# Linear attention and a swish MLP on one core: a hand-made order on all engines, tails in a chunk of their own, a block-diagonal kv and 1 KB loads

## The chip, the cores and the metric

The kernel runs on one core of one Trainium2 chip. The metric is the device time of one execution in microseconds (us). A profile covers a single execution and is some 2 to 4 us shorter than the timed run. All comparisons use runs that the records call fast.

## The reference

Eight batches of eight heads, 576 tokens, 64 channels per head. The attention is linear: a softmax of q over the channels, a softmax of k over the tokens, and `kv = k_s^T v` per head. Its output goes through an MLP with a swish in the middle.

```python
q_s = exp(q - max(q, -1));  q_s /= sum(q_s, -1) + 1e-9
k_s = exp(k - max(k, 2));   k_s /= sum(k_s, 2) + 1e-9
kv  = einsum('bhsd,bhse->bhde', k_s, v)
x   = einsum('bhsd,bhde->bhse', q_s, kv)        # -> (4608, 512)
h   = x @ w_in                                  # (512, 2048)
out = (h * sigmoid(beta * h)) @ w_out           # (2048, 512), float32
```

Both kernels leave out the maximum, work in bf16 on TensorE, and use `sigmoid(z) = (1 + tanh(z/2)) / 2`, so that the gate is one tanh on ScalarE and one `(tanh + 1) * h` on VectorE.

## The kernel before

A batch of 576 tokens is cut into four pieces of 128 and one of 64; the MLP works in nine chunks of 512 tokens, which straddle the batches. The order on each engine is left to the framework's scheduler.

```python
S_CHUNKS = [(0, 128), (128, 128), (256, 128), (384, 128), (512, 64)]

def attention(b):
    for ci, (s0, rows) in enumerate(S_CHUNKS):      # q by SP, k and v by GpSimd; 256 B runs
        nc.sync.dma_start(qt[:rows], q[b, :, s0:s0+rows, :].rearrange("h p d -> p h d"))
    # ... k and v the same way; exp of q and k, row sums and multiplies per 128-token piece ...
    for j in range(HP):                             # two heads at a time
        for ci, (s0, rows) in enumerate(S_CHUNKS):  # the last piece has 64 rows
            nc.tensor.matmul(kvE, Ek[ci][:rows, ...], vaug[ci][:rows, ...], ...)
        # kvp[0:64], kvp[64:128]: the two heads' own 64 x 64 blocks, divided by the column sums
        for ci, (s0, rows) in enumerate(S_CHUNKS):
            nc.tensor.transpose(qsT_ps[:, s0:s0+rows], qs[ci][:rows, ...], identity[:rows, :rows])
        # for the (one or two) pieces of the batch that fall into an MLP chunk, w columns each:
        nc.tensor.matmul(xps[0:D, 0:w], kvp[0:D, :], qsT[0:D, ...], tile_position=(0, 0))
        nc.tensor.matmul(xps[D:P, 0:w], kvp[D:P, :], qsT[D:P, ...], tile_position=(64, 64))
        nc.scalar.copy(xT[c][:, j, off:off+w], xps[:, 0:w])

def mlp_A(c):        # 16 x (4 matmuls into hT, tanh on ScalarE, gate on VectorE)
def mlp_B(c):        # 4 x (16 matmuls into acc, copy on ScalarE, store)

attention(0); issue_weight_dmas(); cast_weights(); mlp_A(0); attention(1); mlp_A(1); mlp_B(0)
for b in range(2, B):
    attention(b); mlp_A(b); mlp_B(b - 1)
mlp_A(NCH - 1); mlp_B(NCH - 2); mlp_B(NCH - 1)
```

The softmax here doesn't subtract the row's maximum and nothing guards it: scores larger than these inputs give would overflow.

Of the kernel before, what the change touches and what calls it, by code (L numbers as in the profile page):

```python
# [9 lines left out]
BF16 = mybir.dt.bfloat16  # L10
F32 = mybir.dt.float32
ALU = mybir.AluOpType
ACTF = mybir.ActivationFunctionType


@with_exitstack
def kernel(
# [16 lines left out]
    NTOK = B * S  # L34
    KT = DM // P
    NJ = FF // P
    CHUNK = 512
    NCH = NTOK // CHUNK
    assert NTOK % CHUNK == 0
    S_CHUNKS = [(0, 128), (128, 128), (256, 128), (384, 128), (512, 64)]  # L40
    NSC = len(S_CHUNKS)
    HP = H // 2

    const = ctx.enter_context(tc.tile_pool(name="const", bufs=1))
    wst = ctx.enter_context(tc.tile_pool(name="wstage", bufs=2))
    stage = ctx.enter_context(tc.tile_pool(name="stage", bufs=3))
    atn = ctx.enter_context(tc.tile_pool(name="atn", bufs=2))
    xtp = ctx.enter_context(tc.tile_pool(name="xt", bufs=1))
    gt = ctx.enter_context(tc.tile_pool(name="gt", bufs=2 * NJ))
    outp = ctx.enter_context(tc.tile_pool(name="outp", bufs=2))  # L50
    psA = ctx.enter_context(tc.tile_pool(name="psA", bufs=1, space=bass.MemoryType.PSUM))
    psM = ctx.enter_context(tc.tile_pool(name="psM", bufs=2, space=bass.MemoryType.PSUM))

    identity = const.tile([P, P], BF16, name="identity")
    make_identity(nc, identity[:])

    beta_t = const.tile([P, NJ], F32, name="beta_t")
    nc.sync.dma_start(beta_t[:], moe_beta.rearrange("(j p) -> p j", p=P))
    beta_half = const.tile([P, NJ], F32, name="beta_half")
    nc.vector.tensor_single_scalar(beta_half[:], beta_t[:], 0.5, ALU.mult)  # L60

    w_in_b = const.tile([P, KT, FF], BF16, name="w_in_b")
    w_out_b = const.tile([P, NJ, DM], BF16, name="w_out_b")
    w_in_dram = moe_w_in.rearrange("(kt p) f -> p kt f", p=P)
    w_out_dram = moe_w_out.rearrange("(j p) f -> p j f", p=P)

    w_stage_in = []
    w_stage_out = []

    def issue_weight_dmas():  # L70
        for i in range(2 * KT):
            kt, half = divmod(i, 2)
            t = wst.tile([P, FF // 2], F32, tag="wst_in", bufs=4, name=f"w_in_st{i}")
            nc.sync.dma_start(
                t[:], w_in_dram[:, kt, half * (FF // 2) : (half + 1) * (FF // 2)]
            )
            w_stage_in.append(t)
        for jj in range(NJ // 4):
            t = wst.tile([P, 4, DM], F32, tag="wst_out", bufs=2, name=f"w_out_st{jj}")
            nc.sync.dma_start(t[:], w_out_dram[:, 4 * jj : 4 * jj + 4, :])  # L80
            w_stage_out.append(t)

    def cast_weights():
        for i in range(2 * KT):
            kt, half = divmod(i, 2)
            nc.vector.tensor_copy(  # L86
                w_in_b[:, kt, half * (FF // 2) : (half + 1) * (FF // 2)], w_stage_in[i][:]
            )
        for jj in range(NJ // 4):
            nc.vector.tensor_single_scalar(  # L90
                w_out_b[:, 4 * jj : 4 * jj + 4, :], w_stage_out[jj][:], 0.5, ALU.mult
            )

    xT = [xtp.tile([P, KT, CHUNK], BF16, name=f"xT{c}") for c in range(NCH)]

    gT_chunks: dict[int, list] = {}

    STAGE_BUFS = 3
    ATN_DEEP = 2 * NSC

    def attention(b: int):
        Ek = []
        qs = []
        vaug = []
        q_st = []
        k_st = []
        for ci, (s0, rows) in enumerate(S_CHUNKS):
            qt = stage.tile([P, H, D], F32, tag="q_st", bufs=NSC)
            nc.sync.dma_start(  # L109
                qt[:rows], q[b, :, s0 : s0 + rows, :].rearrange("h p d -> p h d")  # L110
            )
            q_st.append(qt)
        for ci, (s0, rows) in enumerate(S_CHUNKS):
            kt_ = stage.tile([P, H, D], F32, tag="k_st", bufs=NSC)
            nc.gpsimd.dma_start(
                kt_[:rows], k[b, :, s0 : s0 + rows, :].rearrange("h p d -> p h d")
            )
            k_st.append(kt_)
        for ci, (s0, rows) in enumerate(S_CHUNKS):
            vt = atn.tile([P, H, D + 1], BF16, tag="vaug", bufs=ATN_DEEP)  # L120
            nc.gpsimd.dma_start(  # L121
                vt[:rows, :, 0:D], v[b, :, s0 : s0 + rows, :].rearrange("h p d -> p h d")
            )
            vaug.append(vt)

        for ci, (s0, rows) in enumerate(S_CHUNKS):
            nc.vector.memset(vaug[ci][:rows, :, D : D + 1], 1.0)  # L127
            Eq = atn.tile([P, H, D], BF16, tag="Eq")
            nc.scalar.activation(Eq[:rows], q_st[ci][:rows], ACTF.Exp)  # L129
            qz = atn.tile([P, H], F32, tag="qz")  # L130
            nc.vector.tensor_reduce(  # L131
                qz[:rows], Eq[:rows], axis=mybir.AxisListType.X, op=ALU.add
            )
            rqz = atn.tile([P, H], F32, tag="rqz")
            nc.vector.reciprocal(rqz[:rows], qz[:rows])  # L135
            qst = atn.tile([P, H, D], BF16, tag="qs", bufs=ATN_DEEP)
            nc.vector.tensor_tensor(  # L137
                qst[:rows],
                Eq[:rows],
                rqz[:rows].unsqueeze(2).to_broadcast((rows, H, D)),  # L140
                ALU.mult,
            )
            qs.append(qst)

            Ekt = atn.tile([P, H * D], BF16, tag="Ek", bufs=ATN_DEEP)
            nc.scalar.activation(
                Ekt[:rows, :],
                k_st[ci][:rows].rearrange("p h d -> p (h d)"),
                ACTF.Exp,
            )  # L150
            Ek.append(Ekt)

        col_abs = b * S
        for j in range(HP):
            kvE = psA.tile([P, 2 * (D + 1)], F32, tag="kvE")
            for ci, (s0, rows) in enumerate(S_CHUNKS):
                nc.tensor.matmul(  # L157
                    kvE[:, :],
                    Ek[ci][:rows, ds(P * j, P)],
                    vaug[ci][:rows].rearrange("p h e -> p (h e)")[  # L160
                        :rows, ds(2 * j * (D + 1), 2 * (D + 1))
                    ],
                    start=(ci == 0),
                    stop=(ci == NSC - 1),
                )
            rkz = atn.tile([P, 1], F32, tag="rkz")
            nc.vector.reciprocal(rkz[0:D, :], kvE[0:D, D : D + 1])  # L167
            nc.vector.reciprocal(rkz[D:P, :], kvE[D:P, 2 * D + 1 : 2 * D + 2])
            kvp = atn.tile([P, D], BF16, tag="kvp")
            nc.vector.tensor_scalar(  # L170
                kvp[0:D, :], kvE[0:D, 0:D], rkz[0:D, :], None, op0=ALU.mult
            )
            nc.vector.tensor_scalar(
                kvp[D:P, :], kvE[D:P, D + 1 : 2 * D + 1], rkz[D:P, :], None, op0=ALU.mult
            )

            qsT_ps = psA.tile([P, S], BF16, tag="qsT_ps", bufs=2)
            for ci, (s0, rows) in enumerate(S_CHUNKS):
                nc.tensor.transpose(  # L179
                    qsT_ps[:, s0 : s0 + rows],  # L180
                    qs[ci][:rows].rearrange("p h d -> p (h d)")[:rows, ds(j * P, P)],
                    identity[:rows, :rows],
                )
            qsT = atn.tile([P, S], BF16, tag="qsT")
            nc.vector.tensor_copy(qsT[:, :], qsT_ps[:, :])  # L185

            s_done = 0
            while s_done < S:
                c = (col_abs + s_done) // CHUNK
                off = (col_abs + s_done) % CHUNK  # L190
                w = min(CHUNK - off, S - s_done)
                xps = psA.tile([P, CHUNK], F32, tag="xps")
                nc.tensor.matmul(  # L193
                    xps[0:D, 0:w],
                    kvp[0:D, :],
                    qsT[0:D, s_done : s_done + w],
                    tile_position=(0, 0),
                )
                nc.tensor.matmul(  # L199
                    xps[D:P, 0:w],  # L200
                    kvp[D:P, :],
                    qsT[D:P, s_done : s_done + w],
                    tile_position=(64, 64),
                )
                nc.scalar.copy(xT[c][:, j, off : off + w], xps[:, 0:w])
                s_done += w

    def mlp_A(c: int):
        gts = []
        for j in range(NJ):  # L210
            hT = psM.tile([P, CHUNK], F32, tag="hT")
            for kt in range(KT):
                nc.tensor.matmul(  # L213
                    hT[:, :],
# [82 lines left out]
```

## Time and profile before

| | before |
|---|---|
| timed, median of 3 | 370.23 us (369.5 to 370.23) |
| span of the profile | 366.7 us |
| TensorE busy | 87% |
| MLP matmuls (1152 of 128x512) at the pace of the last stretch, 216 ns | 249 us |

The first lines are from the page of the kernel before. Digits are tenths of a slice of 9.2 us (a 40th of the span): how busy TensorE was, which clock it was granted, and below that what DMA moved in GB/s.

```profile
span 366.7 us, 4552 instructions
...
PE   0125669899998999899989998999999999999995
...
PEclk9999768999999999999999999999999999999999
...
GB/s 187 250 356 327 266 254 241 160 103 219 204 46 188 221 31 78 182 150 27 62 179 115 2 57 93 30 0 57 27 3 57 32 29 2 57 29 29 59 67 76
DMA packets 88486, 41.72 MB, mean 114 GB/s; under 512 B 78480, under 2 KB 78480, under 8 KB 88464
...
```

TensorE is busy in nearly every slice after the ninth, so that 87% says little. What counts is how many MLP matmuls it got through in a stretch. These are the busy times by stretch for instructions that touch `hT` (the first MLP matmul) in the kernel before; the counts in brackets are instructions, the columns are in the first line.

```profile
...
core 0: us, PE busy (x) DVE busy (x) ACT busy (x), PEclk, DMA share, GB/s
0.00:62.00 62.00, 13.99 (x37) 5.31 (x8) 5.36 (x8) 0.89 1.29 270
...
143.00:367.00 224.00, 93.81 (x374) 65.33 (x96) 65.42 (x96) 1.00 0.29 60
...
```

The same for `acc` (the second MLP matmul):

```profile
...
0.00:62.00 62.00, 3.79 (x11) 0.00 (x0) 0.89 1.29 270
...
143.00:367.00 224.00, 108.94 (x435) 16.36 (x28) 1.00 0.29 60
...
```

By 62 us, 37 + 11 = 48 MLP matmuls were done. They need 10 us, so 52 us were lost. From 143 us on it did 809 in 224 us; they need 175. What TensorE waited for, in the kernel before (us in total, times, longest):

```profile
...
PE qsT_ps L179 <- DVE qst L137: 17.8, 5, 9.8
PE hT L213 <- DVE g L225: 12.9, 11, 3.4
...
```

The first, for the softmax of q, lies wholly in the first 62 us. Of the second, for the gate, 4.5 us lie there, with weight casts ahead of the gate in VectorE's queue; 3.0 us follow up to 143 us, and 5.3 us after that.

Late in the kernel TensorE waits little (some 6 of the last 224 us), and still a batch takes 35.05 us, 7.4 more than its 128 MLP matmuls. This is a part of TensorE's timeline there (start, length, instruction; `64*64` is the part of the array that is used):

```profile
...
286.97 0.39 PE L157 MATMUL kvE<-vt,Ekt 128*128 128x130 bf16 x4
287.29 0.21 PE L193 MATMUL xps<-qsT,kvp 64*64 64x64 bf16 x1
...
287.44 0.23 PE L157 MATMUL kvE<-vt,Ekt 64*128 64x130 bf16 x1
287.60 0.40 PE L179 MATMUL qsT_ps<-identity,qst 128*128 128x128 bf16 x4
...
```

Read the starts, not the lengths, which overlap. Four full kv matmuls of 130 columns go from 286.97 to 287.29, 80 ns each on the mean. The fifth, on the 64 rows of the tail, holds 160 ns (287.44 to 287.60), and a pair of x matmuls of only 64 columns 140 to 150 ns.

At both, TensorE changes between the whole array and a part of it.

### The profile page before, as it was taken

How to read it: one execution, taken by the hardware profiler on the slowest of the kernel's cores; microseconds unless marked ns; L12 is line 12 of the kernel's file. 1: busy time of each engine (PE TensorE's matmuls, PEld its weight loads, DVE VectorE, ACT ScalarE, POOL GpSimd, SP SyncE). 2: the span in 40 equal slices, each digit the busy share in tenths (PEclk: the TensorE clock that was granted, in tenths of full speed). 3: DMA queues.
4: the chain of work that ended last, by engine and by line, in shares of the span. 5: the costliest groups of instructions: out<-in, count | busy, mean ns of one | idle time of the engine just before them, and what ended most of it. 6: DMA issues, size and time to landing. Idle time of an engine off the chain costs nothing.

```text
span 366.7 us, 4552 instructions
## 1 busy us (share of the span) xinstructions
PE 317.5 (87%) x1570; PEld 139.3 (38%) x1600; DVE 207.0 (56%) x477; ACT 185.2 (50%) x325; POOL 69.3 (19%) x86
## 2 busy tenths in 40 slices
PE   0125669899998999899989998999999999999995
PEld 0011223443433444344433443345344444444442
DVE  1554736988988937664767566654452545255100
ACT  3312426768668745755485538552554355355211
POOL 8281433035017001800090004000000000000000
PEclk9999768999999999999999999999999999999999
DMA  8999999649719802950293019001001000100111
GB/s 187 250 356 327 266 254 241 160 103 219 204 46 188 221 31 78 182 150 27 62 179 115 2 57 93 30 0 57 27 3 57 32 29 2 57 29 29 59 67 76
DMA packets 88486, 41.72 MB, mean 114 GB/s; under 512 B 78480, under 2 KB 78480, under 8 KB 88464
## 3 DMA queue, kind: packets, MB, share of 16 engines
q0 software_dynamic: 40448, 14.16, 28.8%
q1 hardware_dynamic: 48016, 27.28, 26.3%
q8 instruction: 12, 0.20, 0.2%
q14 instruction: 10, 0.08, 0.1%
HBM read 36.71 MB, written 9.44 MB: 126 GB/s over the span
## 4 chain that ended last, share of the span: by engine, by line
PE 67%; DMA 12%; DVE 11%; issue 4%; ACT 3%; SPq 2%; POOL 1%; ACTq 0%; POOLq 0%
PE hT L213 30%; PE acc L241 27%; DMA qt<-in_q_dram 6%; DMA vt<-in_v_dram 4%; PE kvE L157 4%; PE qsT_ps L179 3%; DVE g L225 3%; PE xps L193 3%; DMA w_in_st_311<-in_moe_w_in_dram 3%; DVE qst L137 2%; SPq L109 2%; DVE qz L131 2%; ACT th L221 1%; DVE w_in_b L86 1%; DVE qsT L185 1%
## 5 line engine op out<-in xcount | busy, mean ns | idle before, releaser
L241 PE MATMUL acc<-w_out_b,g 128*128 128x512 bf16 x561 | 143.8, 381 | 0.6 <-DVE g L225 0.2
L221 ACT ACTIVATE th<-hT,beta_half 128x512 bf16<-128x512 f32 x144 | 97.8, 686 | 72.4 <-PE hT L213 68.8
L225 DVE SCALAR_TENSOR_TENSOR g<-th,hT 128x512 bf16<-128x512 bf16 x144 | 97.7, 685 | 64.8 <-ACT th L221 64.4
L213 PEld LDWEIGHTS <-w_in_b 128*128 128x128 bf16 x576 | 54.4, 98 | 87.3 <-issue 34.4
L241 PEld LDWEIGHTS <-g 128*128 128x128 bf16 x576 | 54.9, 98 | 63.8 <-issue 0.9
L121 POOL DMA_DIRECT2D vt<-in_v_dram x40 | 33.9, 871 | 121.6 <-DVE qz L131 101.8
L249 ACT COPY o_sb<-acc 128x512 f32<-128x512 f32 x36 | 21.0, 584 | 44.6 <-PE acc L241 41.1
L179 PE MATMUL qsT_ps<-identity,qst 128*128 128x128 bf16 (+1 forms) x160 | 18.8, 226 | 19.1 <-DVE qst L137 17.8
L131 DVE TENSOR_REDUCE qz<-Eq 128x8 f32<-128x512 bf16 (+1 forms) x40 | 26.8, 671 | 13.3 <-ACT Eq L129 8.7
L129 ACT ACTIVATE Eq<-qt 128x512 bf16<-128x512 f32 (+1 forms) x40 | 25.0, 627 | 11.0 <-DMA qt<-in_q_dram 8.5
L137 DVE TENSOR_TENSOR qst<-Eq,rqz 128x512 bf16<-128x512 bf16 (+1 forms) x40 | 27.1, 684 | 2.6 <-DVE rqz L135 1.9
L157 PE MATMUL kvE<-vt,Ekt 128*128 128x130 bf16 (+1 forms) x160 | 20.9, 232 | 7.8 <-DVE vt L127 7.2
L213 PE MATMUL hT<-xT_93,w_in_b 128*128 128x512 bf16 x63 | 20.7, 469 | 6.0 <-DVE g L225 5.8
L193 PE MATMUL xps<-qsT,kvp 64*64 64x512 bf16 (+7 forms) x64 | 20.2, 316 | 3.9 <-DVE kvp L170 2.6
L179 PEld LDWEIGHTS <-qst 128*128 128x128 bf16 (+1 forms) x160 | 11.1, 99 | 27.3 <-DVE qst L137 19.6
L199 PE MATMUL xps<-qsT,kvp 64*64 64x512 bf16 (+7 forms) x64 | 20.3, 317 | 0.3 <-issue 0.3
L167 DVE RECIPROCAL rkz<-kvE 64x1 f32<-64x1 f32 x32 | 5.0, 158 | 27.3 <-PE kvE L157 26.5
L157 PEld LDWEIGHTS <-Ekt 128*128 128x128 bf16 (+1 forms) x160 | 12.4, 100 | 19.6 <-issue 10.7
L213 PE MATMUL hT<-xT_96,w_in_b 128*128 128x512 bf16 x63 | 16.4, 378 | 2.0 <-DVE g L225 2.0
L213 PE MATMUL hT<-xT_97,w_in_b 128*128 128x512 bf16 x63 | 16.5, 378 | 1.6 <-DVE g L225 1.6
L213 PE MATMUL hT<-xT_94,w_in_b 128*128 128x512 bf16 x62 | 16.4, 380 | 0.9 <-DVE g L225 0.8
L213 PE MATMUL hT<-xT_95,w_in_b 128*128 128x512 bf16 x62 | 16.2, 379 | 1.1 <-DVE g L225 0.9
(121 smaller groups left out, 222.7 us busy)
## 6 DMA issues: line engine op xcount, KB each, us to landing
out_dram<-o_sb SPq DMA_DIRECT2D x36, 256.0 KB, 2.0
qt<-in_q_dram SPq DMA_DIRECT2D x32, 256.0 KB, 5.4
vt<-in_v_dram POOLq DMA_DIRECT2D x32, 128.0 KB, 5.6
qt<-in_q_dram SPq DMA_DIRECT2D x8, 128.0 KB, 6.1
w_out_st_315<-in_moe_w_out_dram SPq DMA_DIRECT2D x1, 1024.0 KB, 12.0
w_out_st_317<-in_moe_w_out_dram SPq DMA_DIRECT2D x1, 1024.0 KB, 14.9
w_out_st_319<-in_moe_w_out_dram SPq DMA_DIRECT2D x1, 1024.0 KB, 10.7
w_out_st_321<-in_moe_w_out_dram SPq DMA_DIRECT2D x1, 1024.0 KB, 11.8
```

The source lines that it names most:

```text
L121: nc.gpsimd.dma_start(vt[:rows, :, 0:D], v[b, :, s0 : s0 + rows, :].rearrange("h p d -> p h d"))
L129: nc.scalar.activation(Eq[:rows], q_st[ci][:rows], ACTF.Exp)
L131: nc.vector.tensor_reduce(qz[:rows], Eq[:rows], axis=mybir.AxisListType.X, op=ALU.add)
L137: nc.vector.tensor_tensor(qst[:rows], Eq[:rows], rqz[:rows].unsqueeze(2).to_broadcast((rows, H, D)), ALU.mult,)
L157: nc.tensor.matmul(kvE[:, :], Ek[ci][:rows, ds(P * j, P)], vaug[ci][:rows].rearrange("p h e -> p (h e)")[:rows, ds(2 * j * (D + 1), 2 * (D ...
L179: nc.tensor.transpose(qsT_ps[:, s0 : s0 + rows], qs[ci][:rows].rearrange("p h d -> p (h d)")[:rows, ds(j * P, P)], identity[:rows, :rows],)
L193: nc.tensor.matmul(xps[0:D, 0:w], kvp[0:D, :], qsT[0:D, s_done : s_done + w], tile_position=(0, 0),)
L213: nc.tensor.matmul(hT[:, :], w_in_b[:, kt, ds(j * P, P)], xT[c][:, kt, :], start=(kt == 0), stop=(kt == KT - 1),)
L221: nc.scalar.activation(th[:, :], hT[:, :], ACTF.Tanh, scale=beta_half[:, j : j + 1])
L225: nc.vector.scalar_tensor_tensor(out=g[:, :], in0=th[:, :], scalar=1.0, in1=hT[:, :], op0=ALU.add, op1=ALU.mult,)
L241: nc.tensor.matmul(acc[:, :], gts[j][:, ds(st * P, P)], w_out_b[:, j, :], start=(j == 0), stop=(j == NJ - 1),)
L249: nc.scalar.copy(o_sb[:, :], acc[:, :])
```

## The change

The intent is to keep TensorE on MLP matmuls from as early as possible. The parts:

- **Order.** All engines run in program order, written by hand. A unit is one group of first MLP matmuls (four of 512 columns) with tanh and gate; the second MLP matmuls follow two units later. The next batch's attention is put into fixed units of a chunk.
- **Tokens.** Each batch gives a chunk of 512 tokens; the eight tails of 64 tokens make the ninth chunk. Partition p holds the tokens 4p to 4p+3, so q, k and v come in runs of 1 KB, all on the SP queue.
- **kv.** Two heads' kv are kept as a 128 x 128 matrix with zeros off the diagonal blocks, so that x is one full matmul. The tails of two batches share 128 rows; zeros in `vt` keep them apart. The factor 1/2 of the sigmoid, before in w_out's cast and in beta, is now in the column of v that sums k (2 instead of 1).
- **Weights and v.** Weights are loaded and cast in 1 MB blocks in order of need; w_out's casts move from VectorE to GpSimd, w_in's stay on VectorE. v, which the load itself cast before, now comes as float32 and is cast by GpSimd (batch 0's by VectorE).
- **Warm-up.** 36 dummy matmuls at the start.

```diff
+    R = 4; MAIN = R * P; TAIL = S - MAIN; LAG = 2
+    ctx.enter_context(tc.manual_schedule())
+    def main_view(t, b):
+        return t[b, :, 0:MAIN, :].rearrange("h (p i) d -> p h (i d)", i=R)
 ...
+    def kv_mm(b, jj):                       # the tail's part: 128 rows, half of them meet zeros
+            nc.tensor.matmul(t[:, jl, :], ekt[:, pr, ds(j * P, P)], vt[:, pr, e, ...],
+                             start=False, stop=True)
 ...
-                nc.tensor.matmul(xps[0:D, 0:w], kvp[0:D, :], qsT[0:D, ...], tile_position=(0, 0))
-                nc.tensor.matmul(xps[D:P, 0:w], kvp[D:P, :], qsT[D:P, ...], tile_position=(64, 64))
+            nc.tensor.matmul(t[:], kvp[:, c, j, :], qsT[c][:, :, j, :])
 ...
+    load_main(q_st, q, 0, "q_st", parts=2)
+    load_main(k_st, k, 0, "k_st", parts=2)
+    load_tail(kt_st, k, 0, "kt_st", es=(0,)); load_tail(vt_st, v, 0, "vt_st", es=(0,))
+    load_main(v_st, v, 0, "v_st", parts=2)
+    nc.sync.dma_start(beta_t[:], moe_beta.rearrange("(j p) -> p j", p=P))
+    w_load("in", 0); w_load("out", 0); w_load("in", 1)   # ... and so on, in order of need
 ...
+    for s in range(2):
+        v_cast(0, nc.vector, s, 2)
+    w_cast("in", 0, nc.vector)
+    for jj in range(2):
+        kv_mm(0, jj); kv_norm(0, jj)
+    for j in range(HP):
+        x_mm(0, j, nc.scalar if j % 2 == 0 else nc.vector)
+    nc.gpsimd.memset(kvp[:, 1:B], 0.0)      # and va[1], vt of the later batches
 ...
+    def side(c, u):                         # attention of the next batch, by unit u of chunk c
+            off = {0: "q0", 1: "q1", 2: "k0", 3: "k1", 5: "qT", 7: "kv0", 9: "kv1"}   # c > 0
 ...
+    for n in range(len(units) + LAG):
+        if n < len(units):
+            mm_a(*units[n])
+        if n >= LAG:
+            cb, jb = units[n - LAG]
+            mm_b(cb, jb)
+            if jb == NJ - 1:
+                store(cb)
+        if n < len(units):
+            side(*units[n])
```

## The prediction

> **What bounds it now.** The profile spans 366.7 us (timed 370.2: some 3.5 us outside). TensorE is busy for 87%; in the chain of waits it has 67%, DMA 12%, VectorE 11%. In the last stretch of the timeline 16 MLP matmuls take 3.45 us, 216 ns each; 1152 need 249 us, a floor that the change leaves. The other 118 us (MLP matmuls counted by stretch):
> - 0 to 62 us: 48 MLP matmuls (10 us), 52 us lost. TensorE waits for the softmax of q, v, and g behind weight casts; granted clock 0.66 from 40 to 60 us. DMA moves 199 GB/s in the first 10 us, but 323 to 366 between 20 and 36 us. 78,480 of 88,486 packets are under 512 B. The Trainium skill ("DMA: Bandwidth & Descriptors", Specifications) wants 512 B for line rate; the trace agrees in direction.
> - 62 to 143 us: 269 (58 us), 23 us lost.
> - 143 us to the end: 49 us lost; 35 to 37.5 us per batch where 128 MLP matmuls need 27.6.
>
> **What changes.**
> - q, k, v load in 1 KB runs, by need. I expect 310 to 340 GB/s from about 2 us on.
> - Attention on TensorE: 160 transposes become 144, kv stays 160 (about 83 ns each in the trace); 128 half-array x matmuls (pairs 0.33 us at 512 columns, 0.15 at 64) become 32 full ones of 216 ns and 32 small. Per batch 5.3 us plus switches and gaps (7.4 in all) becomes about 4.2 (estimate).
> - Tanh and gate (0.69 us each, 144 of each) stay. The second MLP matmul follows two units behind, so their 1.5 us has about 2.6: slack 1.1 us.
> - Added: v and w_out casts on GpSimd. From the Trainium skill ("GPSIMD Engine Reference", 3.1: 1.03 to 1.8 cycles per element at 1.2 GHz) I estimate 2 to 3 us per 2048 elements; this trace has no such cast.
> - Accumulators fill four banks, so each chunk change waits for evacuations (0.58 us each): about 1 us. VectorE is overfull in a chunk's first four units (8.4 us of work in 6.9), eating most of the slack.
>
> **Sum.**
> - MLP starts near 22 us (q, k, v, tails, first weight block: 4.5 MB); 2 us more for a cold clock.
> - Chunk 0 is DMA-paced: 15 MB until v of batch 1, landing at 50 to 53 us, then a 3 us cast; TensorE reaches that kv near 52. Chunk 0 ends near 61 us.
> - Chunks 1 to 6: 27.6 + 4.2 + 1 = 32.8 us each, to 258. Chunk 7: 32.8; chunk 8: 28.7: to 320. Last evacuations and stores: 2 to 4.
> - Span about 322, timed 325. Startup gives about 21 us, the rest comes from the period of a batch.
>
> All of it lies on TensorE's path.
>
> **Prediction: 325 us, 8 in 10 between 313 and 340. Faster by over 2%: 0.97; within 2%: 0.02; slower: 0.01.**
>
> **What would show each step.** First MLP matmul at 20 to 24 us. Over 300 GB/s in the first slices. TensorE idle over 3 us near the end of chunk 0, for kv of batch 1 (v cast). From chunk 1 on a period of 32 to 33.5 us, with about 1 us idle at the accumulators' change, behind VectorE. x matmuls at about 216 ns. Clock below 1 only in the first 35 us.
>
> **What would make it wrong.** GpSimd casts far over 3 us, or locking VectorE (chunk 0 longer by 5 to 15 us). VectorE's backlog stalling TensorE in every chunk (2 us times eight). Staging buffers holding up loads. Or the other way: chunk 0 nearly without stalls and a period of 31.5 us, giving 312.

## The result, and the profile after

| | before | after |
|---|---|---|
| timed, median of 4 | 369.88 us | 321.74 us (320.69 to 323.17) |
| ratio | | 0.8707 [0.8675, 0.8739] |
| span of the profile | 366.7 us | 319.0 us |
| first MLP matmul of chunk 1 | | 60.57 us |
| period of a chunk, from 92 to 219 us | | 31.6 us |

A ratio is the mean time of one kernel's fast runs over that of the other's fast runs of the same rounds, so it isn't quite the ratio of the medians quoted here. The brackets are 95% intervals. The kernel before had medians from 368.9 to 370.4 us, so ratios are the safer comparison between rounds.

The page of the changed kernel, the same lines as before:

```profile
span 319.0 us, 4013 instructions
...
PE   8539999889999999999999999999999999999990
...
PEclk9955999999999999999999999999999999999996
...
GB/s 238 190 277 379 307 358 352 267 200 329 7 0 193 280 121 0 197 329 2 2 217 270 109 0 239 290 0 0 193 72 2 0 133 0 2 17 116 2 0 132
DMA packets 46931, 46.40 MB, mean 145 GB/s; under 512 B 15680, under 2 KB 40256, under 8 KB 46912
...
```

The packets have fallen from 88,486 to 46,931. TensorE is full from the fourth slice on, and its granted clock is at half speed in slices three and four (16 to 30 us), where the first MLP matmuls fall.

TensorE's waits in the changed kernel (each tile has its own line here):

```profile
...
PE kv_0_246 L218 <- DVE va_73 L147: 4.7, 1, 4.7
PE tp_2_226 L201 <- DVE qs_207 L182: 3.7, 1, 3.7
...
PE acc_1_1905 L291 <- DVE o_1882 L250: 0.7, 1, 0.7
...
PE kv_0_538 L218 <- POOL va_74 L147: 0.2, 1, 0.2
...
```

The first two lines are the start. The third is one of seven alike, 0.73 us each: the change of accumulators between two chunks. The last is what I had expected to be over 3 us: the kv of batch 1, at the end of chunk 0.

Where the start goes, in the timeline of the changed kernel (SPq is the DMA queue of SyncE):

```profile
...
11.98 4.63 SPq L118 DMA_DIRECT2D w_in_105<-in_moe_w_in_dram  x1
...
14.78 3.08 POOL L364 MEMSET kvp<- 128x3584 bf16 x1
...
17.08 4.73 DVE L147 CAST va_73<-v_st_101 128x1024 bf16<-128x1024 f32 x2
...
17.86 2.77 POOL L366 MEMSET vt<- 128x3120 bf16 x1
...
21.73 1.23 DVE L125 CAST w_in_b<-w_in_105 128x2048 bf16<-128x2048 f32 x1
...
```

Two things stand out. The two casts of v on VectorE took 4.73 us together, and while they did, GpSimd was in two long memsets; the first cast alone lasted 4.1 us and ended half a microsecond after the second memset. And the issue of the first weight block was held for 4.63 us. Here are stretches of that time (the last two numbers are the DMA share and GB/s):

```profile
...
core 0: us, PE busy (x) PEld busy (x) DVE busy (x) ACT busy (x) POOL busy (x), PEclk, DMA share, GB/s
...
14.00:15.00 1.00, 0.00 (x0) 0.00 (x0) 0.96 (x2) 0.13 (x1) 0.77 (x2) 1.00 0.87 101
15.00:16.00 1.00, 0.03 (x1) 0.03 (x2) 0.92 (x1) 0.00 (x0) 1.00 (x1) 1.00 0.31 43
16.00:17.00 1.00, 0.59 (x8) 0.42 (x8) 0.59 (x2) 0.00 (x0) 1.00 (x1) 0.86 0.13 8
17.00:18.00 1.00, 0.00 (x0) 0.00 (x0) 1.00 (x2) 0.00 (x0) 1.00 (x3) 0.50 0.38 39
18.00:20.00 2.00, 0.00 (x0) 0.00 (x0) 2.00 (x1) 0.00 (x0) 2.00 (x2) 0.50 0.97 370
...
```

Between 14 and 18 us DMA moved only 8 to 101 GB/s, a few microseconds after the load of beta was issued (at 9.90); beta landed 7.7 us after its issue. After that hole, up to 32 us, it moves 360 to 398 GB/s. The column before the last two is the granted clock: half speed from 17 us on.

The kv matmuls of one pair of heads in a later chunk of the changed kernel, to set beside those of before:

```profile
...
108.41 0.39 PE L218 MATMUL kv_0_1082<-va_74,ek_976 128*128 128x130 bf16 x4
108.63 0.22 PE L225 MATMUL kv_0_1082<-vt,ekt 128*128 128x130 bf16 x1
108.69 0.39 PE L218 MATMUL kv_0_1082<-va_74,ek_976 128*128 128x130 bf16 x4
108.92 0.22 PE L225 MATMUL kv_0_1082<-vt,ekt 128*128 128x130 bf16 x1
...
```

Ten matmuls in 0.56 us (two of them on the tails' shared rows), 56 ns each, and no change of array form. Before, the tail alone held 160 ns.

The change of accumulators between two chunks in the changed kernel:

```profile
...
95.35 1.22 DVE L174 TENSOR_REDUCE rq_930<-eq_928 128x16 f32<-128x1024 bf16 x1 [0.26 <-ACT eq_928 L161]
...
96.78 0.63 DVE L279 SCALAR_TENSOR_TENSOR g_1_940<-th_1_938,h_1_933 128x512 bf16<-128x512 bf16 x1
...
97.32 0.68 DVE L250 COPY o_946<-acc_1_659 128x512 f32<-128x512 f32 x1
...
98.05 0.38 PE L291 MATMUL acc_1_967<-w_out_b,g_0_922 128*128 128x512 bf16 x1 [0.74 <-DVE o_946 L250]
...
```

VectorE takes the row sum first (95.35, waiting for its exponential), then the gate (96.78), and only at 97.32 evacuates the second accumulator, which TensorE needs from 97.3 on (98.05 less the 0.74 us in the brackets). ScalarE had evacuated the first by 96.6.

And the end of the changed kernel:

```profile
...
311.12 5.02 SPq L307 DMA_DIRECT2D out_dram<-o_2993  x8
...
```

The last matmul is over at 311.1 us; from then on SP issues eight stores for 5.02 us, and the kernel ends at 319.0.

**Where the 48 us came from.** At 60.57 us the changed kernel had done 64 + 56 = 120 MLP matmuls, from its timeline; the kernel before had done 48 by 62 us. The 72 more are worth 72 x 0.216 = 15.6 us, and it was there 1.4 us earlier: 17 us from the start. The other 31 us come from the later part: 1032 matmuls in 258.4 us after, 1104 in 304.7 us before. That is 35 and 66 us above their 216 ns each. Of the 17 us, the longer runs give 7 to 8 (u_256 below); how the rest divides among the order of the loads, the move of k and v from GpSimd's queue to SP's, and the casts, no run took apart.

### The profile page after: what moved, and what is told of

It is laid out like the page before. It is cut to its first block, busy times and chain, and to the rows that moved or that the text cites. A ratio compares the mean times of both kernels' runs of the same rounds, so it can differ in the third digit from the quotient of the medians.

```text
span 319.0 us, 4013 instructions
## 1 busy us (share of the span) xinstructions
PE 291.1 (91%) x1529; PEld 139.0 (44%) x1556; DVE 197.1 (62%) x324; ACT 153.9 (48%) x220; POOL 38.4 (12%) x41
## 4 chain that ended last, share of the span: by engine, by line
PE 73%; DVE 13%; DMA 3%; ACT 3%; issue 3%; POOL 1%; DVEq 0%; SPq 0%; ACTq 0%; POOLq 0%
DMA v_st_127<-in_v_dram 3%; DVE va_73 L147 1%; DVE w_in_b L125 1%; PE acc_1_2809 L291 1%; PE acc_2_2810 L291 1%; PE acc_3_2524 L291 1%; PE acc_1_2522 L291 1%; PE acc_2_2523 L291 1%; PE acc_0_2808 L291 1%; PE acc_0_2521 L291 1%; PE acc_3_2811 L291 1%; PE acc_1_967 L291 1%; PE acc_1_1282 L291 1%; PE acc_1_1590 L291 1%; PE acc_1_2213 L291 1%
## 5 line engine op out<-in xcount | busy, mean ns | idle before, releaser
L343 PEld LDWEIGHTS <-warm 128*128 128x128 bf16 x36 | 4.0, 114 | 7.3 <-issue 3.3
L147 POOL CAST va_73<-v_st_1690 128x2048 bf16<-128x2048 f32 x1 | 1.9, 1918 | 33.5 <-PE acc_3_1592 L291 33.5
L174 DVE TENSOR_REDUCE rq_204<-eq_202 128x16 f32<-128x1024 bf16 x2 | 2.4, 1214 | 5.6 <-ACT eq_202 L161 5.6
L147 POOL CAST va_73<-v_st_1067 128x2048 bf16<-128x2048 f32 x1 | 1.9, 1919 | 33.0 <-DMA v_st_1067<-in_v_dram 33.0
L255 PEld LDWEIGHTS <-kvp 128*128 128x128 bf16 x32 | 3.0, 99 | 5.4 <-DVE kvp L239 2.1
L147 POOL CAST va_74<-v_st_1377 128x2048 bf16<-128x2048 f32 x1 | 1.9, 1922 | 25.3 <-PE kv_1_1433 L218 25.3
L147 POOL CAST va_74<-v_st_2000 128x2048 bf16<-128x2048 f32 x1 | 1.9, 1917 | 23.8 <-DMA v_st_2000<-in_v_dram 23.8
L147 DVE CAST va_73<-v_st_101 128x1024 bf16<-128x1024 f32 x2 | 4.7, 2404 | 0.0
L131 ACT ACTIVATE ek_238<-k_st_94 128x1024 bf16<-128x1024 f32 x2 | 2.1, 1056 | 4.3 <-DMA k_st_94<-in_k_dram 4.3
L125 POOL CAST w_out_b<-w_out_117 128x2048 bf16<-128x2048 f32 x1 | 2.8, 2812 | 8.3 <-DMA w_out_117<-in_moe_w_out_dram 8.3
L161 ACT ACTIVATE eq_202<-q_st_91 128x1024 bf16<-128x1024 f32 x2 | 2.1, 1056 | 2.9 <-DMA q_st_91<-in_q_dram 2.9
L147 POOL CAST va_74<-v_st_754 128x2048 bf16<-128x2048 f32 x1 | 1.9, 1918 | 12.3 <-DMA v_st_754<-in_v_dram 12.3
L225 PEld LDWEIGHTS <-ekt 128*128 128x128 bf16 x32 | 3.3, 104 | 0.0
L147 POOL CAST va_73<-v_st_603 128x2048 bf16<-128x2048 f32 x1 | 1.9, 1917 | 10.9 <-DMA v_st_603<-in_v_dram 10.9
L364 POOL MEMSET kvp<- 128x3584 bf16 x1 | 3.1, 3077 | 0.0
L182 DVE TENSOR_TENSOR qs_207<-eq_202,rq_204 128x1024 bf16<-128x1024 bf16 x2 | 2.9, 1431 | 0.1
L182 DVE TENSOR_TENSOR qs_666<-eq_618,rq_620 128x1024 bf16<-128x1024 bf16 x2 | 2.8, 1405 | 0.0
```

The source lines that it names most:

```text
L125: eng.tensor_copy(dst, wst[kind, blk][:])
L131: nc.scalar.activation(ek[b][:, :, s * m : (s + 1) * m, :].rearrange("p i h d -> p h i d"), k_st[b][:, s * m : (s + 1) * m, :].rearrange(" ...
L147: eng.tensor_copy(va[b % 2][:, :, s * m : (s + 1) * m, 0:D].rearrange("p i h d -> p h i d"), v_st[b][:, s * m : (s + 1) * m, :].rearrange( ...
L174: nc.vector.tensor_reduce(rq[b][:, 0, :, h], eq[b][:, :, h, :], axis=AX.X, op=ALU.add)
L182: nc.vector.tensor_tensor(qs[b][:, :, h, :], eq[b][:, :, h, :], rq[b][:, 1, :, h].unsqueeze(3).to_broadcast((P, R, m, D)), ALU.mult,)
L225: nc.tensor.matmul(t[:, jl, :], ekt[:, pr, ds(j * P, P)], vt[:, pr, e, 2 * j : 2 * j + 2, :].rearrange("p h d -> p (h d)"), start=False, s ...
```

## The experiments

All of these change the changed kernel (321.74 us, ratio 0.8707). All gave correct results. In the first five (u_) one part of the change is undone; the others (e_) go after what the prediction had wrong.

### u_256: runs of 256 B again

```diff
-        return t[b, :, 0:MAIN, :].rearrange("h (p i) d -> p h (i d)", i=R)
+        return t[b, :, 0:MAIN, :].rearrange("h (i p) d -> p h i d", i=R)    # four loads; stores to match
```

> The changed kernel with q, k and v loaded in 256 B runs again (four loads per tensor and batch, token order changed to match; stores in 2 KB runs). My theory: runs matter only while TensorE waits for data, that is until v of batch 1 lands (53.0 us in the changed kernel); 6.3 MB of q, k, v lie before that, and at 200 instead of 340 GB/s they cost up to 13 us more. So 328 to 336 us, with the period of later chunks still 31.6 us. Rival: the old kernel was paced by loads throughout, and most of the 48 us comes from the 1 KB runs: then 345 us or more and longer periods in every chunk.

Measured: 329.69 us (329.49 to 330.3), ratio 0.8908 [0.8855, 0.8962]. The later period stays at 31.6 us (the accumulator changes lie at 106.79, 138.38, 169.98 and 201.57 us in its timeline). The cast of v of batch 1 starts at 61.9 us, not 53.1, and TensorE waits another 4.5 us for casts of w_in. So the long runs matter while data are short, in the first 60 us, and give about 7 to 8 of the 48 us. The rival falls. The run also has four times as many loads of q, k and v, but the DMA engines were busy throughout while they moved less, so that the cost lies in the packets and not in waiting for issues. A stretch of the changed kernel, then the same one of u_256 (the last two numbers are the DMA share and GB/s; up to 16 us u_256 goes on with 1.10 and 214, then 1.26 and 196):

```profile
...
4.00:8.00 4.00, 4.00 (x15) 1.50 (x14) 2.29 (x3) 2.11 (x2) 0.00 (x0) 1.00 0.98 321
...
4.00:8.00 4.00, 4.00 (x20) 1.73 (x19) 0.29 (x1) 2.58 (x3) 0.00 (x0) 1.00 1.05 231
...
```

The trace agrees in direction with the 512 B that the Trainium skill ("DMA: Bandwidth & Descriptors", Specifications) asks for.

### u_halfx: x in two 64 x 64 matmuls

```diff
-            nc.tensor.matmul(t[:], kvp[:, c, j, :], qsT[c][:, :, j, :])
+            for e in range(2):
+                r = slice(e * D, (e + 1) * D)
+                nc.tensor.matmul(t[r, :], kvp[r, c, j, e*D:(e+1)*D], qsT[c][r, :, j, :],
+                                 tile_position=(64 * e, 64 * e))
```

> The changed kernel with each x matmul of a main chunk done as two 64 x 64 matmuls in the two quarter arrays (tile positions 0,0 and 64,64) as in the old kernel, without use of the zero blocks. My theory: the pair takes 0.33 us where the full one takes 0.216, so 0.12 us times four per batch plus some switching cost: period 32.1 to 32.6 us, 325 to 329 us in all. Rival: the two halves run side by side and the block-diagonal form gives nothing: within 1 us of the changed kernel (321.7).

Measured: 326.07 us (325.68 to 327.07), ratio 0.881 [0.8745, 0.8875], and a period of 32.48 us. TensorE's timeline in this run:

```profile
...
114.50 1.03 PE L296 MATMUL acc<-w_out_b,g 128*128 128x512 bf16 x4
115.46 0.40 PE L257 MATMUL x<-qsT,kvp 64*64 64x512 bf16 x2
115.79 1.04 PE L274 MATMUL h<-xT,w_in_b 128*128 128x512 bf16 x4
...
```

The four acc matmuls end at 114.50 + 0.86 = 115.36. The x pair starts 0.1 us later, and the next group at 115.79: the pair holds 0.43 us where a full matmul holds 0.216. Four times the difference is 0.86 us, and the period rose by 0.88. The expectation holds. The rival is right that the two halves run side by side (they start 3 ns apart); the time goes into the step before the pair (0.1 us more than the 216 ns) and the one after it.

### u_tail64: the tail's kv on 64 rows

```diff
-                ekt[:, pr, ds(j * P, P)],      vt[:, pr, e, ...]
+                ekt[ds(e * TAIL, TAIL), pr, ds(j * P, P)],   vt[ds(e * TAIL, TAIL), pr, e, ...]
```

> The changed kernel with the tail's kv matmul on the 64 rows of its own batch instead of 128 rows half of which meet zeros. In the old trace the matmuls on 64 rows stand about 0.16 us apart, the full ones 0.06 to 0.08. Theory: four of these per batch, 0.1 us more each, so the period rises by 0.3 to 0.5 us and the time to 324 to 326 us. Rival: rows don't matter, only columns do: unchanged, within 0.7 us.

Measured: 327.2 us (326.86 to 328.76), ratio 0.8846 [0.879, 0.8903], period 32.43 us: a miss upwards. Its timeline:

```profile
...
109.80 0.39 PE L218 MATMUL kv<-va,ek 128*128 128x130 bf16 x4
110.12 0.23 PE L225 MATMUL kv<-vt,ekt 64*128 64x130 bf16 x1
110.28 0.40 PE L218 MATMUL kv<-va,ek 128*128 128x130 bf16 x4
...
```

Five matmuls now take 0.48 us (109.80 to 110.28), not 0.28. So one matmul on half of the rows costs 0.2 us more than the same on all rows with half of them zero: it starts late (110.12, not 110.03) and holds the next one up (0.16 us, not 0.06). Four per batch make the 0.83 us by which the period rose. I had put 0.1 us on each. Unmerged, the four full ones still stand 57 ns apart; the time is in the two changes, 0.15 us before the half-row matmul and 0.16 after it where 0.06 would do.

### u_unint: the MLP not interleaved

```diff
-        for n in range(len(units) + LAG):  mm_a(unit n); mm_b(unit n - LAG); side(unit n)
+    for c in range(NCH):
+        for hf in range(2):
+            for j in range(8 * hf, 8 * hf + 8):  mm_a(c, j); side(c, j)
+            for j in range(8 * hf, 8 * hf + 8):  mm_b(c, j)
+        store(c)
```

(With ten buffers for g instead of five, and one for the output instead of two.)

> The changed kernel with the MLP not interleaved: eight first matmul groups, then their eight second groups (more buffers for g, one for the output). My theory: in a run of first groups two PSUM buffers must pass through tanh and gate (1.5 us per two groups and matmul), so a group takes 1.25 us instead of 0.86, and VectorE has to do a unit's attention work in that time too (about 12.6 us of work in the first eight units, which TensorE could do in 7): 5 to 10 us per chunk, 365 to 405 us in all, so that the whole gain is gone. Rival: interleaving is not needed, because the two halves of a chunk overlap in any order as in the old kernel: under 335 us.

Measured: 370.85 us (370.28 to 372.45), ratio 1.0024 [0.9961, 1.0088]: no faster than the kernel before, with everything else of the change in place. TensorE's waits in it:

```profile
...
PE h L269 <- DVE g L279: 30.9, 54, 1.3
...
```

TensorE waits 54 times for a gate that frees a PSUM buffer of h; in the changed kernel such waits come to 0.2 us. These waits are 30.9 of the 49 us; the rest I didn't trace. This shows that in this order the rest of the change gains nothing. It doesn't show that the interleaving alone is worth 49 us, because the old kernel's scheduler did interleave to a degree: the period of a chunk is 37.1 us here, longer than the 35.05 of the kernel before.

### u_lag1: the second matmuls one unit behind

```diff
-    LAG = 2
+    LAG = 1
```

> The changed kernel with the second MLP matmuls one unit behind the first instead of two. Theory: tanh and gate then have 1.73 us for their 1.5, a slack of 0.2 instead of 1.1 us, so each attention instruction of VectorE or ScalarE of over a microsecond (row sums, multiplies, exponentials in a chunk's first four units) stalls TensorE: 2 to 4 us more per chunk, 335 to 350 us. Rival: the slack isn't needed, since two PSUM buffers for h set the distance anyway: under 2 us in all.

Measured: 327.21 us (325.9 to 329.36), ratio 0.8869 [0.8809, 0.8929], period 32.3 us. Theory and rival both miss: it costs more than 2 us, but far less than 14. In its trace there is one stall of 0.85 us per chunk, at the second unit's accumulation, where the gate stands behind a row sum (1.0 us from start to start, and one of 0.2 us follows; 8.7 us in twelve waits, chunk 0 with them). On the other side, a chunk's accumulators are now evacuated a unit earlier, before VectorE is in the row sums, and that wait falls from 0.73 to 0.16 us. So the slack of 0.2 us was enough for most of VectorE's attention work, and my count of stalls was too large.

### e_mem, e_beta and e_membeta: what sets the start

```diff
 # e_mem
+    nc.gpsimd.memset(kvp[:, 1:B], 0.0)      # with the other memsets: now ahead of the v tail's cast
 ...
-    nc.gpsimd.memset(kvp[:, 1:B], 0.0)      # was: behind it
 # e_beta
+    nc.sync.dma_start(beta_t[:], moe_beta.rearrange("(j p) -> p j", p=P))    # first of all loads
     load_main(q_st, q, 0, "q_st", parts=2)
 ...
-    nc.sync.dma_start(beta_t[:], moe_beta.rearrange("(j p) -> p j", p=P))    # was: before w_load("in", 0)
```

> The changed kernel with GpSimd's long memsets (kvp, vt of the later batches) placed before the wait for the first v tail, so that they are over by about 12 us. In the changed kernel the first of VectorE's two v casts took 4.1 us and ended 0.5 us after the 2.77 us memset of vt, the second 0.7 us. Theory: GpSimd holds VectorE up for its whole instruction; now both casts take about 0.7 us. But the first weight block lands only at 21.4 us, so the first MLP matmul moves by only about 0.4 us from 26.8 and the time by at most 1 us (320.7 to 321.7). Rival 1: the cast is slow for its strided rows, and stays at over 2 us. Rival 2: the casts alone set the start, and the time falls by 3 us or more.

> The changed kernel with the load of beta (2048 elements of 4 B each to its own place) issued first instead of just ahead of the first weight block. In the changed kernel it took 7.7 us to land, and the next issue was held for 4.6 us while 8 to 100 GB/s were moved from 14 to 18 us; in the old kernel, issued first, it landed in 2.9 us. Theory: the hole goes, and the first weight block lands 3 us earlier, near 18 us. But the v casts still end at 21.8 us, so by itself this moves the first MLP matmul by under 1 us: 320.5 to 322 us. Rival: the loads alone set the start, and the time falls by 3 us or more.

> Both of these edits. Theory: the v casts behind memsets and the weight block behind beta end within 0.4 us of each other, so only both together bring the start forward: first MLP matmul at 23 to 24 us instead of 26.8, the later loads follow (their issue waits for casts that follow TensorE), and the time falls by 2.5 to 4 us, to about 318.5, more than the sum of the two single edits. Rival: chunk 0 is bound by the total of bytes, whatever the start: under 1 us.

Measured:

| | median of 6, us | ratio | first MLP matmul |
|---|---|---|---|
| changed kernel | 321.74 (of 4) | 0.8707 | 26.8 us |
| e_mem | 320.63 (320.09 to 321.21) | 0.8684 [0.8653, 0.8715] | 25.6 us |
| e_beta | 321.52 (320.65 to 323.07) | 0.8714 [0.8678, 0.875] | 26.0 us |
| e_membeta | 318.79 (317.38 to 321.3) | 0.8645 [0.8604, 0.8685] | 23.4 us |

The timeline of e_mem, with the casts of v and the cast of the weight block:

```profile
...
16.46 1.29 DVE L147 CAST va<-v_st 128x1024 bf16<-128x1024 f32 x2
...
20.49 1.23 DVE L125 CAST w_in_b<-w_in 128x2048 bf16<-128x2048 f32 x1 [2.74 <-DMA w_in<-in_moe_w_in_dram]
...
```

Both casts of v now take 1.29 us together instead of 4.73, so the long time was GpSimd's memsets and not the strided rows. (In the eight traces of fast runs with the memsets in the late place the first cast takes 2.95 to 5.35 us, in the four with early memsets 0.7.) But VectorE then sits idle for 2.74 us until the weight block lands, and the kv norm stands behind that cast in its order. In e_beta DMA's hole from 14 to 18 us is gone (366 to 388 GB/s from 14 to 20 us; a smaller one is now at the start, 70 GB/s from 2 to 4 us where the changed kernel moved 303), but the casts of v take 4.42 us as before. Only with both do both ends come forward, here in the timeline of e_membeta:

```profile
...
16.00 1.29 DVE L147 CAST va<-v_st 128x1024 bf16<-128x1024 f32 x2
...
18.34 1.23 DVE L125 CAST w_in_b<-w_in 128x2048 bf16<-128x2048 f32 x1 [1.04 <-DMA w_in<-in_moe_w_in_dram]
...
```

First MLP matmul 3.4 us earlier than in the changed kernel's trace, and about 2.3 us less time by the ratio (0.0062 x 370). The single edits give 0.9 and nothing. The sizes are unsure. The timed intervals of e_mem and e_membeta overlap, and that of e_membeta touches the changed kernel's. And a trace is one execution: in four traces whose program is the same up to the first MLP matmul it starts at 23.7 (u_lag1), 25.3 (u_unint), 26.1 (e_shift) and 26.8 us (the changed kernel), because the first loads land at other times. So the 25.6 and 26.0 us of the single edits show no gain, and the 23.4 us with both lies only just below that spread; e_best and e_fill below, which have both edits too and a further one at the start, begin at 22.45 and 22.30. What the traces do show directly is which of the two waits ends last in each kernel.

### e_shift: the row sums away from the accumulator change

```diff
-            off = {0: "q0", 1: "q1", 2: "k0", 3: "k1", 5: "qT", 7: "kv0", 9: "kv1"}
+            off = {2: "q0", 3: "q1", 4: "k0", 5: "k1", 6: "qT", 8: "kv0", 9: "kv1"}
```

(Cut: q's multiplies and transposes, moved to match.)

> The changed kernel with the q softmax of the next batch moved from the first four units of a chunk to units 2 to 5 (transposes one unit later), so that VectorE isn't busy with the row sum when the accumulators have to be evacuated. Theory: the wait of 0.73 us at each accumulator change falls to 0.2 to 0.45 us and nothing else gets worse: period 31.2 to 31.3 instead of 31.6 us, 318.5 to 320 us in all. Rival: the wait is set by the evacuations themselves, four of 0.6 us on two engines, and stays at 0.7 us: no change within 0.7 us.

Measured: 316.45 us (316.12 to 317.77), ratio 0.8573 [0.8539, 0.8607], period 31.00 us. More than expected; in its waits the accumulator change is down to 0.16 us each, 1.3 us in all where it was 5.3:

```profile
...
PE acc L291 <- DVE o L250: 1.3, 8, 0.2
...
```

### e_nowarm: no warm-up matmuls

```diff
-WARM = 36
+WARM = 0
```

> The changed kernel without its 36 warm-up matmuls. In its trace they end at 11.65 us, hold up the first transposes by 3 us, and the clock falls to half again from 16 to 30 us, in the wait for v, so that the first three MLP groups run at half speed anyway. Theory: they gain nothing: within 1 us of 321.7. Rival: they are what makes the start fast, and without them the time rises by 3 us or more.

Three of four runs: 320.11, 320.82 and 322.33 us, ratio 0.8694 [0.8639, 0.8748]. So the dummies gain nothing measurable (there is no trace of a fast run). The fourth run took 1065.26 us, and the profile fell on it; it counts as slow. From its page:

```profile
span 1063.0 us, 3968 instructions
...
```

Over the whole execution its MLP matmuls stood about 0.85 us apart, four times 216 ns. The page has no line for the granted clock: no change of it was recorded. This happened in no other run. Whether it has to do with the missing warm-up or with that one execution of the chip, a single run can't tell; it stays open.

### e_best and e_fill: all that gained, in one kernel

e_best is e_mem, e_beta and e_shift, and two more edits:

```diff
-    w_cast("in", 0, nc.vector)
+    w_cast("in", 0, nc.gpsimd)
 ...
-                    nc.sync.dma_start(out[r0 : r0 + TAIL, :], ...)      # the last chunk's eight stores, all issued after the four evacuations
+                    (nc.sync if e == 0 else nc.scalar).dma_start(out[r0 : r0 + TAIL, :], ...)
```

> All that gained, in one kernel: memsets early, beta first, the softmax shifted by two units; and two small edits: the first weight block is cast by GpSimd (so that VectorE is free for the kv norm), and the last eight stores are issued half from SP, half from ScalarE (in the changed kernel SP takes 5.0 us to issue them, and 7.9 us pass between the last matmul and the end). Theory: minus 3 us (start), minus 4.8 (period 31.0), minus 2 (end): 310 to 313 us. Rival: the gains at the start and in the period overlap, and it stays at 314 us or more.

Measured: 312.19 us (311.41 to 314.88), ratio 0.8462 [0.8421, 0.8503]. It beats both kernels: 15% less than before, 3% less than the change. First MLP matmul at 22.45 us, period 31.0 us. From the last matmul to the end there are 6.7 us instead of 7.9, so that the split of the stores gave 1.2 us and not the 2 expected. What the cast on GpSimd gave by itself, no run shows.

e_fill adds ten dummy matmuls (`fill(10, ...)`) after batch 0's transposes and four (`fill(4, ...)`) before its x matmuls.

> The same with 14 more dummy matmuls, ten after the transposes of batch 0 and four ahead of its x matmuls, so that TensorE doesn't go idle before the first MLP matmul. Theory: the clock stays full, twelve first MLP matmuls at 216 instead of 427 ns, up to 2.5 us less than without, as far as the loads of chunk 0 allow: 308 to 311.5 us. Rival: chunk 0 then waits for its weights or for v of batch 1, and nothing is gained: within 0.7 us of the kernel without them.

Measured: 312.85 us (312.59 to 314.88), ratio 0.8487 [0.8448, 0.8527]. The clock now stays full in the whole start, and the time doesn't fall. TensorE's waits for w_in's casts show why: 3.5 us in all (the longest 2.1), where in e_best they are 1.6. The faster matmuls run into the loads. The rival was right here.

## Why the prediction was right

The prediction was 325 us, between 313 and 340; it became 321.74. The span was predicted at about 322 and came to 319.0. Point by point:

- **What bounds it: right.** TensorE's stream is the end of nearly every wait. 1152 matmuls at 216 ns stayed the floor, and undoing one part costs what it takes on TensorE: 0.88 us per chunk for the half-array x, 0.83 for the half-row tail. What I had not seen is that both are the same cost, of changes between the whole array and a part of it.
- **Interleaving with two units of slack: right in kind.** Without it the whole gain is gone (u_unint, ratio 1.0024). But the size of the slack matters less than I had argued: with 0.2 us instead of 1.1 a chunk loses 0.7 us (u_lag1).
- **"MLP starts near 22 us": too early.** It was 26.8 us, at half clock until 30. "Over 300 GB/s in the first slices" was wrong too: 238, 190 and 277, although from 2 to 8 us it was 303 to 323. (The 199 GB/s that I gave for the runs of 256 B hold a quiet start, 33 GB/s up to 4 us; 196 to 231 in u_256 is the better figure.) The term I had left out is two waits that end together: VectorE's cast of v behind GpSimd's memsets, and the first weight block behind the load of beta. In the traces taking away either moves the start by 0.8 to 1.2 us, both together by 3.4 (e_mem, e_beta, e_membeta), with the spread between executions told there.
- **"TensorE idle over 3 us near the end of chunk 0": wrong.** It waited 0.24 us for that kv. v of batch 1 landed at 53.0 us, as predicted (50 to 53), and GpSimd cast it in 1.92 us (predicted 3). But chunk 0 isn't paced by DMA alone: loads are issued when casts and activations, which follow TensorE, free the buffers. In e_membeta, which starts 3.4 us earlier, the same cast begins at 49.56 us instead of 53.10, and TensorE waits 0.54 us; in no trace is this wait over 1.6 us. So the date of v, and with it the end of chunk 0 (60.57 us, predicted 61), came out right by luck: the start was late, and no stall of 3 us followed.
- **"A period of 32 to 33.5 us": too long.** It was 31.6. The term that was mis-sized is attention on TensorE: transposes and kv take 56 ns each, not the 83 taken from the old trace. Those 83 came from groups that had half-row or half-array matmuls in them: in u_tail64, too, four full ones before a half-row one take 0.32 us, as in the old trace, and 0.22 without it. Unmerged, full ones stand 57 ns apart in the old trace as well; the rest was the change of array form, which this change takes away. Sixteen transposes and twenty kv at 27 ns less are 1.0 us per batch. The change of accumulators cost 0.73 us, predicted about 1, and behind VectorE, as e_shift shows.
- **"Last evacuations and stores: 2 to 4" us: too short.** It was 7.9 us, since SP issues the last eight stores one after another in 5.0 us.
- **Sum.** By the sum's own marks chunk 0 ended 0.4 us early, chunks 1 to 6 took 190.0 us instead of 196.8, chunk 7 30.5 instead of 32.8. Chunk 8 and the end took 37.9 us instead of some 31.5. The total came out right because these errors were small and had both signs, which is luck: the period of 31.5 us, with which I had gone down to 312, came true, and the later end made up for it.

What isn't shown by a run: how the remaining 1.7 us of the late period (35.05 to 31.6, less 0.88 and 0.83) divide among fewer transposes, those on 64 rows, and fewer pieces of x. The old trace points to the changes of array form again: 27 in a batch, some 3 us, of which u_halfx and u_tail64 each bring back eight (0.84 and 0.81 us in their traces). The other eleven, of the transposes on 64 rows and the second pieces of x, come to over a microsecond (estimate). The changed kernel has none in a main chunk.

## What to carry to other kernels

Put a producer of work far enough ahead in TensorE's own order that ScalarE and VectorE finish behind it, and keep the long instructions of those engines away from the moments when TensorE has to get a buffer back; here the first was worth 15% of the changed kernel's time and the second 1.5%. Keep every matmul on the whole array and fill the unused rows with zeros: going to a part of the array and back costs 0.2 us each time (here; whether several such matmuls in a row share that cost was seen only for x pairs, which do). The zeros themselves cost memsets of 2.8 and 3.1 us on GpSimd, and here these held up VectorE's first cast. When two waits end within a microsecond of each other, removing either may show nothing; remove both before you call them harmless, and compare more than one trace of a start.

## What the Trainium skill lacked or had wrong

- "TensorE: Matmul & The Clock Gate", Back-to-back issue gap, gives about 81 ns per matmul of 128 columns in a stream of weight loads and matmuls, and about 131 ns at 512 columns, and calls some 56 and 216 ns those of an isolated matmul. Here streams with a weight load before each matmul ran at 56 ns (130 columns, ten in 0.56 us) and 216 ns, which fits the second pair of figures and not the first. The 80 ns of the old trace are the mean of steps of 57 ns and one change of array form.
- No page gives the time of a change between the whole array and a part of it; "TensorEngine Tiling (Array Packing)", Key Properties, says that changing the tiling mode drains TensorE, without a figure. Here each change took about 0.1 us: 0.2 us for a half-row matmul among full ones (u_tail64) and 0.22 us for an x pair (u_halfx).
- "SBUF — State Buffer", Who interferes with whom, says that GpSimd or a VectorE instruction in a two-port mode, whichever is first, gets the shared ports for a whole instruction. The traces agree, and add that VectorE can lose twice in a row: its cast was due at 17.08 us, and a memset that began at 17.86 went before it (4.1 us instead of 0.69 in e_mem).
- "DMA: Bandwidth & Descriptors", Rules for kernel authors, says that a strided last dimension becomes one descriptor per element; no page says what such a load costs the loads behind it. Beta (8 KB in elements of 4 B) landed in 7.7 us, the next issue took 4.6 us, and 8 to 101 GB/s were moved from 14 to 18 us; issued first, it took 0.45 us of issue and landed in 2.9 us, with 70 GB/s moved from 2 to 4 us.
- "GPSIMD Engine Reference", 3.1: its 1.03 to 1.8 cycles per element would be 1.76 to 3.07 us for 2048 elements (estimate); in the changed kernel casts from float32 to bf16 took 1.89 to 1.92 us, and 2.81 us once beside a VectorE cast. The page fits at its lower end; section 3.1 times no cast.
- "TensorE: Matmul & The Clock Gate" notes a clock seen stuck at a quarter for 50 us and more. One run of e_nowarm ran at a quarter of the pace throughout, 1063 us, while the recorded mean clock was 1.000 and the page has no line for the clock.
